# Grouped-query attention on one core: V in 8 KB pieces, 32-row score tiles, 64x64 PV tiles, and a longer TensorE loop

## The chip, the core and the metric

The kernel runs on one core of one Trainium2 chip. The metric is device time in microseconds (us), the median of a few runs. One further execution was recorded by the profiler; its record (the trace, summed up in the page of the profile) is what durations and waits are read from. The engines are PE (TensorE matmuls; PEld its weight loads), DVE (VectorE), ACT (ScalarE), POOL (GpSimd) and SP (SyncE, which here only issues DMAs). Sixteen DMA engines move the data.

## The reference

There are 16 batches, 32 query heads, 8 key/value heads, 16 queries a head, 2048 keys, head size 128, all in bf16. Four query heads share one key/value head.

```python
k = jnp.repeat(k, 4, axis=1); v = jnp.repeat(v, 4, axis=1)
scores = jnp.einsum("bhqd,bhkd->bhqk", q, k) * D ** -0.5
p = softmax(scores, axis=-1)
out = jnp.einsum("bhqk,bhkd->bhqd", p, v)
```

So 128 key/value heads (16 x 8) each meet 64 query rows (4 heads x 16 queries). K and V are 67.1 MB each; q and the output are 2.1 MB each.

## The kernel before, in words

**Tiling.** Four key/value heads make a quad Q (32 quads). K comes by quad, 2 MB at a time, 16 KB in each of 128 partitions (`load_k`, L311). V comes by pair of heads p (64 pairs), 1 MB at a time, as two runs of 4 KB in each partition, one for each head of the pair (`load_v`, L318). The work goes in 64 steps. Step n handles one half of the keys (1024) of all four heads of quad n//2 as far as the scores go, and one pair of heads as far as exp and PV go.

**What a step does on each engine.**
- DVE turns K by 32x32 blocks, two STREAM_TRANSPOSEs a step (`kt`, L558-566), which gives the tile KT; there are two KT buffers. It then reads the scores out of PSUM, scales and negates them, and takes the row minimum on the way (`negated`, L571-579), two instructions a step. At odd steps it also makes the exp bias (L581), at even steps a reciprocal (L568).
- PE computes the scores S(n) (`scores`, L391-406): 16 matmuls of 512 columns in tiles of 64 rows by 128 columns. The weights hold q for two heads with zeros where head and key do not belong together; two tiles run side by side. The four PSUM banks of S_ps hold one step only, so S(n) waits for `negated` of step n-1 (`sem_max`) and for KT (`sem_kt`).
- ACT takes exp (L674), one instruction of 128x2048 a pair, and copies the turned probabilities out of PSUM (L683), two a pair.
- PE turns the probabilities of a pair by eight 128x128 transposes in two halves (`p_turn`, L410: "PT"), and multiplies by V ("PV", L429 for the helper in the loop, L483 and L489 outside). A pair with an even number is done as 16 matmuls with 128x128 weights and 256 moving columns, of which half is thrown away (`both_heads`); an odd one as 32 matmuls in 128x64 tiles with 128 columns.
- ACT scales the result and writes it to SBUF (L697, L701: "norm"); SP stores it (L344).

**Queries.** q is laid out by POOL with a mask (L255, 28 parts), turned by PE in float32 (L392, four transposes a part) and copied by ACT (L664). Inside the loop, POOL also copies a quad's part to a fixed place (L294).

**The order.** PE's order is written out: PV(p-4), PT(p-2), S(p+2), and at every second step a part of q. PE and DVE run loops on the chip: PE 23 turns of two steps (L509, registers computed at the head of a turn: L510-521, waits L525-526), DVE 9 turns of six steps. ACT's program is straight. SP issues in one order (L351-367): at t, K of quad t/2 if t is even (after the K buffer three quads back was turned), V of pair t-6 (after PV of pair t-14; from pair 50 on one t later, `VLATE`), and the store of pair t-14. There are 3 K buffers and 8 V buffers. V of the last pair comes in two pieces (keys 0-11 and 12-15 of each partition's 16).

**The end.** The last five pairs are scaled by DVE (L655) and the last four use banks of S_ps, so that the last exps, PTs and PVs follow one another closely (L206-217).

Of the kernel before, what the change touches and what calls it, by code (L numbers as in the profile page):

```python
# [12 lines left out]
NV = 8  # L13
# [3 lines left out]
NO = 12  # L17
NOG = 4
NQ = 2
NSTAGE = 3  # L20
VLAG = 6
VLATE = 50
PVLAG = 4
SLAG = 14
QLOAD = (0, 1, 5)
QLEAD = 13
QAHEAD = 6
LOOP = (3, 26)
QUNIT = 2
EVBASE = 4  # L30
NMBASE = 6
QTBASE = 1
Q4BASE = 1
VBASE = 16
HEAD = 40
RING = 6
VLOOP = (3, 30)
VHEAD = 140
EXPBASE = 3
LASTV = ((0, 12), (12, 16))  # L40
NFAST = 8
NLATE = 5


def both_heads(p, NP):
    return p < NP - NFAST and p % 2 == 0


def bass_standalone__gqa_softmax__sampling_kernel(
# [10 lines left out]
    G = B * Hkv  # L60
    NP = G // 2
    NQD = NP // 2
    J = Sk // 128
    assert J == 16 and NP % 8 == 0
    NQC = NP // 8
# [6 lines left out]
    ident4 = sb("ident4", [128, 128], F32)  # L72
    mask = sb("mask", [128, 4], F32)
    Kn = [sb(f"Kn{i}", [128, 4 * J * 128], BF16) for i in range(NK)]
    v_base = -(-nc.sbuf_base // 32) * 32
    Vb = sb("Vb", [128, NV, 2, J, 128], BF16)
    KT = [sb(f"KT{i}", [128, 2 * J * 64], F32) for i in range(NKT)]
    Qn = [sb(f"Qn{i}", [128, 8, 128], BF16) for i in range(NQ)]
    Q4 = sb("Q4", [128, 4, 4, 4, 64], BF16)
    QTq = Q4[:, 3, :, :, :].rearrange("p j r c -> p (j r c)").rearrange("p (b n e) -> p b n e", b=2, e=2)  # L80
    QT = [sb(f"QT{i}", [128, 2, 1024], F32) for i in range(2)]
    Sneg = [sb(f"Sneg{i}", [128, Sk], F32) for i in range(NS)]
    P = [sb(f"P{i}", [128, Sk // 2], F32) for i in range(2)]
    PT = [sb(f"PT{i}", [128, J // 2, 128], F32) for i in range(NPT)]
    Osb = [sb(f"O{i}", [128, 128], BF16) for i in range(NO)]
# [11 lines left out]
    def o_done(p):  # L97
        return sem_o[p // NOG % (NO // NOG)], 16 * NOG * (p // NO)

# [4 lines left out]
    iota_m = iota_m.bitcast(I32)  # L104

    S_ps = ctx.enter_context(nc.psum_tensor("S_ps", [128, Sk], F32))
    ST_ps = ctx.enter_context(nc.psum_tensor("ST_ps", [128, NSTAGE * 512], F32))
    O_ps = ctx.enter_context(nc.psum_tensor("O_ps", [128, 512], F32))
# [3 lines left out]
    sem_v = [sem(f"sem_v{i}") for i in range(NV)]  # L112
    sem_vl = [sem(f"sem_vl{i}") for i in range(2)]
    sem_q = [sem(f"sem_q{i}") for i in range(NQ)]
    sem_o = [sem(f"sem_o{i}") for i in range(NO // NOG)]
    sem_kt = sem("sem_kt")
    sem_qa = sem("sem_qa")
    sem_qb = sem("sem_qb")
    sem_q4 = sem("sem_q4")
    sem_qt = sem("sem_qt")  # L120
    sem_qe = sem("sem_qe")
    sem_max = sem("sem_max")
# [3 lines left out]
    sem_stq = sem("sem_stq")  # L126
# [3 lines left out]
    sem_ev = [sem(f"sem_ev{i}") for i in range(2)]  # L130
    sem_nm = sem("sem_nm")
# [5 lines left out]
    vf = v.rearrange("b h s d -> (b h) (s d)").rearrange("g (a x) -> a g x", a=128)  # L137

    pe_prog, act_prog = [], []
    M0, M1 = LOOP  # L140
    NQP = 4 * NQC
    assert M0 >= QUNIT and M1 % 2 == 0 and M1 + QAHEAD <= NQP
    bank_used = [None] * NSTAGE

    def pe_op(*op):
        pe_prog.append(op)

    def q_part(k):
        pe_op("Q", k)
        act_prog.append(("qe", k))  # L150

    def turn(j):
        for h in range(2):
            pe_op("PT", j, h)
            act_prog.append(("pe", j, h))

    def pt_slot(p):
        return p % 2 if p < 2 * M1 - 2 else p % NPT

    for k in range(4):  # L160
        q_part(k)
    pe_op("S", 0)
    pe_op("S", 1)
    for p in range(2 * M1):
        if p == 2 * M0:
            pe_op("loop")
        m, h = divmod(p, 2)
        if p >= 4:
            pe_op("PV", p - 4)
            act_prog.append(("norm", p - 4))  # L170
        act_prog.append(("exp", p))
        if p >= 2:
            turn(p - 2)
        pe_op("S", p + 2)
        if m < QUNIT:
            for k in ((4,), (5,), (6, 7), ())[p]:
                q_part(k)
        elif h == 0:
            q_part(m + QAHEAD)
    pe_op("end")  # L180

    p = 2 * M1
    turn(p - 2)
    pe_op("S", p + 2)
    act_prog.append(("exp", p))
    pe_op("PV", p - 4)
    act_prog.append(("norm", p - 4))
    turn(p - 1)
    if M1 + QAHEAD < NQP:
        q_part(M1 + QAHEAD)  # L190
    p += 1
    pe_op("S", p + 2)
    act_prog.append(("exp", p))
    pe_op("PV", p - 4)
    act_prog.append(("norm", p - 4))
    turn(p - 1)
    turn(p)
    for p in range(2 * M1 + 2, NP - 2):
        pe_op("S", p + 2)
        act_prog.append(("exp", p))  # L200
        pe_op("PV", p - 4)
        act_prog.append(("norm", p - 4))
        turn(p)
        if p % 2 == 0 and p // 2 + QAHEAD < NQP:
            q_part(p // 2 + QAHEAD)
    for p in range(NP - 2 - PVLAG, NP - NLATE):  # L206
        pe_op("PV", p)
        act_prog.append(("norm", p))
    act_prog.append(("exp", NP - 2))
    act_prog.append(("exp", NP - 1))  # L210
    for p in range(NP - NLATE, NP - 3):
        pe_op("PV", p)
    turn(NP - 2)
    pe_op("PV", NP - 3)
    turn(NP - 1)
    pe_op("PV", NP - 2)
    pe_op("PV", NP - 1)

    banks, stage_of, free_of = 0, {}, {}
    for op in pe_prog:  # L220
        if op[0] not in ("Q", "PT"):
            continue
        if op[0] == "Q":
            bank, done = (op[1] % NSTAGE if op[1] < 4 else 2), ("q", op[1] + 1)
            banks = 0
        elif op[1] < max(NP - 8, 2 * M1 - 2):
            bank, done = op[2], (op[2], EVBASE + op[1] + 1)
        else:
            bank, done = banks % NSTAGE, (op[2], EVBASE + op[1] + 1)
            banks += 1  # L230
        stage_of[op], free_of[op] = bank, bank_used[bank]
        bank_used[bank] = done

    def stage_ap(op):
        return ST_ps[:, 512 * stage_of[op]:512 * (stage_of[op] + 1)]

    def copies(n):
        return QUNIT < n <= M1

    def o_ap(p):  # L240
        if p < NP - 4:
            return O_ps[:, 0:128]
        x = p - (NP - 4)
        return S_ps[:, 512 * x:512 * x + 128]

    def q_wide(c):
        return Qn[c % NQ][:, :, :].rearrange("p j (b x) -> p b j x", b=2)

    def lay_part(eng, k):
        c, i = divmod(k, 4)  # L250
        b, x = divmod(i, 2)
        src = q_wide(c)[:, b, 4 * x:4 * (x + 1), :].unsqueeze(2).to_broadcast([128, 4, 4, 64])
        by = mask[:, :].unsqueeze(1).unsqueeze(3).to_broadcast([128, 4, 4, 64])
        region = i if c < 2 else 0
        return eng.tensor_tensor(Q4[:, region, :, :, :], src, by, op=ALU.mult)  # L255

    with nc.Block() as block:

        @block.gpsimd
        def _(gp):  # L260
# [15 lines left out]
            def part(k):  # L276
                c, i = divmod(k, 4)
                if i == 0:
                    gp.wait_ge(sem_q[c % NQ], 16 * (c // NQ + 1))
                gp.wait_ge(sem_stq, k - 3 if c < 2 else 5 if k == 8 else k)  # L280
                ins = lay_part(gp, k)
                if c < 2:
                    ins.then_inc(sem_qb, 1)
                else:
                    ins.then_inc(sem_q4, 1 + (Q4BASE if k == 8 else 0))

            def copy(n):
                c, i = divmod(n, 4)
                gp.wait_ge(sem_s, 2 * n)
                if i == 0 or n == QUNIT + 1:  # L290
                    gp.wait_ge(sem_qe, 4 * c + 4)
                if n == QUNIT + 1:
                    gp.wait_ge(sem_stq, 8)
                gp.tensor_copy(  # L294
                    QTq[:, :, :, :].rearrange("p b n e -> p b (n e)").bitcast(I32),
                    QT[c % 2][:, :, 256 * i:256 * (i + 1)].bitcast(I32),
                ).then_inc(sem_qt, 1 + (QTBASE if n == QUNIT + 1 else 0))

            for k in range(4, QUNIT + QAHEAD + 1):
                part(k)  # L300
            copy(QUNIT + 1)
            for m in range(QUNIT, M1):
                if m + QAHEAD + 1 < NQP:
                    part(m + QAHEAD + 1)
                if copies(m + 2):
                    copy(m + 2)
            for k in range(M1 + QAHEAD + 1, NQP):
                part(k)

        @block.sync  # L310
        def _(sp):  # L311
            def load_k(n):
                s = n % NK
                if n >= NK:
                    sp.wait_ge(sem_kt, 4 * (n - NK) + 4)
                sp.dma_start(Kn[s][:, :], kf[n]).then_inc(sem_k[s], 16)  # L316

            def load_v(p):  # L318
                s = p % NV
                if p >= NV:  # L320
                    sp.wait_ge(sem_pv, p - NV + 1)
                if p < NP - 1:
# [28 lines left out]
            for t in range(NP + SLAG + 1):  # L351
# [14 lines left out]
                if 0 <= t - SLAG < NP:  # L366
                    store(t - SLAG)
# [363 lines left out]
```

## Time and profile before

| what | before |
|---|---|
| median of 3 runs | 338.88 us (338.87 to 341.11) |
| the profiled execution, its own time | 338.73 us |
| its span, first to last instruction | 336.9 us |
| K's turns, DVE L562 | 128 x 1219 ns = 151.0 us busy |
| `negated`, DVE L573 | 128 x 1207 ns = 150.1 us busy |
| exp, ACT L674 | 64 x 2002 ns = 128.1 us busy |
| PSUM copies of PT, ACT L683 | 128 x 590 ns = 68.8 us busy |
| mean DMA rate | 411 GB/s |
| instruction fetches, queue q8 | 8 packets, 0.13 MB |

"Busy" counts the time in which an instruction of the group ran; the mean of one is the duration of one instruction, and where two tiles run side by side the mean of one matmul is longer than the distance from one to the next. The span is 1.83 us shorter than the profiled execution's own time. The profile gives for each group of instructions its idle time before it and what ended that, and a view of stretches of time gives each engine's busy time in them. In the text, "neg" is `negated`, and "E61" is the moment when neg of step 61 has ended, 315.5 us in this trace.

### The profile page before, as it was taken

How to read it: one execution, taken by the hardware profiler on the slowest of the kernel's cores; microseconds unless marked ns; L12 is line 12 of the kernel's file. 1: busy time of each engine (PE TensorE's matmuls, PEld its weight loads, DVE VectorE, ACT ScalarE, POOL GpSimd, SP SyncE). 2: the span in 40 equal slices, each digit the busy share in tenths (PEclk: the TensorE clock that was granted, in tenths of full speed). 3: DMA queues.
4: the chain of work that ended last, by engine and by line, in shares of the span. 5: the costliest groups of instructions: out<-in, count | busy, mean ns of one | idle time of the engine just before them, and what ended most of it. 6: DMA issues, size and time to landing. Idle time of an engine off the chain costs nothing.

```text
span 336.9 us, 7946 instructions
## 1 busy us (share of the span) xinstructions
PE 299.8 (89%) x3264; PEld 172.9 (51%) x2752; DVE 304.7 (90%) x457; ACT 245.9 (73%) x376; POOL 69.7 (21%) x64
## 2 busy tenths in 40 slices
PE   3466899999999999999998998889898879999885
PEld 3012456655566555665555456455465445555564
DVE  1788999999999999999998999989899999999941
ACT  3124887888888898888876877767867787877873
POOL 2802022221222222222122222022221200000000
PEclk9998999999999999999999999999999999999999
DMA  7999999999999999999999999999999999999996
GB/s 294 443 413 431 414 410 408 418 424 426 420 413 413 423 424 422 417 411 421 426 427 416 410 417 424 425 418 422 409 422 425 430 416 424 418 411 416 413 412 226
DMA packets 32670, 138.60 MB, mean 411 GB/s; under 512 B 10896, under 2 KB 11152, under 8 KB 28560
## 3 DMA queue, kind: packets, MB, share of 16 engines
q1 hardware_dynamic: 32656, 138.42, 100.6%
q8 instruction: 8, 0.13, 0.2%
q14 instruction: 6, 0.05, 0.0%
HBM read 136.31 MB, written 2.10 MB: 411 GB/s over the span
## 4 chain that ended last, share of the span: by engine, by line
DMA 39%; PE 32%; DVE 21%; ACT 3%; issue 2%; SPq 2%; DVEq 0%; ACTq 0%
DMA Kn<-in_k_dram 25%; DMA Vb<-in_v_dram 14%; DVE Sneg L573 11%; DVE KT L562 10%; PE O_ps L429 9%; PE S_ps L406 8%; PE S_ps L376 7%; PE ST_ps L414 6%; PE ST_ps L392 2%; ACT P L674 1%; SPq L349 1%; ACT PT L683 1%; ACT QT L664 0%; PE S_ps L489 0%; SPq L316 0%
## 5 line engine op out<-in xcount | busy, mean ns | idle before, releaser
L562 DVE STREAM_TRANSPOSE KT<-Kn 128x1024 f32<-128x1024 f32 x128 | 151.0, 1219 | 9.0 <-DMA Kn<-in_k_dram 9.0
L573 DVE TENSOR_SCALAR_CACHE_REDUCE Sneg<-S_ps 128x1024 f32<-128x1024 f32 x128 | 150.1, 1207 | 8.5 <-PE S_ps L376 8.4
L674 ACT ACTIVATE P<-Sneg,nbias 128x2048 bf16<-128x2048 f32 x64 | 128.1, 2002 | 31.7 <-DVE nbias L582 15.7
L255 POOL TENSOR_TENSOR Q<-Qn,mask 128x1024 bf16<-128x1024 bf16 x28 | 52.9, 1894 | 135.4 <-PE ST_ps L392 128.9
L429 PE MATMUL O_ps<-Vb,PT 128*64 (+1 forms) x1104 | 68.8, 238 | 11.3 <-DMA Vb<-in_v_dram 10.2
L406 PE MATMUL S_ps<-KT,Q 64*128 64x512 bf16 x384 | 74.8, 386 | 0.0
L376 PE MATMUL S_ps<-KT,Q 64*128 64x512 bf16 x384 | 74.2, 383 | 0.0
L429 PEld LDWEIGHTS O_ps<-Vb,PT 128*64 128x64 bf16 (+1 forms) x1104 | 55.6, 106 | 35.2 <-issue 27.9
L683 ACT ACTIVATE PT<-ST_ps 128x512 f32<-128x512 f32 x128 | 68.8, 590 | 3.0 <-PE ST_ps L414 2.2
L414 PE MATMUL ST_ps<-ident,P 128*128 128x128 f32 x512 | 68.2, 276 | 1.5 <-ACT PT L683 1.2
L414 PEld LDWEIGHTS ST_ps<-ident,P 128*128 128x128 f32 x512 | 56.3, 141 | 5.9 <-ACT P L674 2.2
L697 ACT ACTIVATE O<-O_ps,rrec 64x128 bf16<-64x128 f32 x56 | 20.3, 362 | 38.2 <-PE O_ps L429 30.9
L406 PEld LDWEIGHTS S_ps<-KT,Q 64*128 64x128 bf16 x384 | 18.6, 93 | 49.7 <-issue 38.2
L406 PE MATMUL S_ps<-KT,QT 64*128 64x512 bf16 x128 | 28.2, 423 | 13.5 <-DVE Sneg L573 9.8
L392 PEld LDWEIGHTS ST_ps<-ident,Q 128*128 128x128 f32 x128 | 15.2, 153 | 25.4 <-issue 25.4
L376 PE MATMUL S_ps<-KT,QT 64*128 64x512 bf16 x128 | 28.2, 422 | 0.0
L392 PE MATMUL ST_ps<-ident,Q 128*128 128x128 f32 x128 | 22.2, 306 | 6.6 <-DVE Q L605 5.4
L294 POOL COPY Q<-QT 128x512 int32<-128x512 int32 x24 | 14.6, 610 | 58.8 <-PE S_ps L376 58.8
L664 ACT ACTIVATE QT<-ST_ps 128x512 f32<-128x512 f32 x32 | 19.3, 603 | 9.8 <-PE ST_ps L392 9.8
L406 PEld LDWEIGHTS S_ps<-KT,QT 64*128 64x128 bf16 x128 | 7.7, 99 | 34.1 <-issue 29.5
L701 ACT ACTIVATE O<-O_ps,rrec 128x128 bf16<-128x128 f32 x31 | 11.7, 378 | 2.4 <-PE O_ps L489 2.3
L674 ACT ACTIVATION_READ_ACCUMULATOR P<-Sneg,nbias 128x1 f32 x64 | 12.0, 188 | 0.0
(25 smaller groups left out, 71.6 us busy)
## 6 DMA issues: line engine op xcount, KB each, us to landing
Kn<-in_k_dram SPq DMA_DIRECT2D x32, 2048.0 KB, 18.6
Vb<-in_v_dram SPq DMA_DIRECT2D x63, 1024.0 KB, 16.9
Qn<-in_q_dram SPq DMA_DIRECT2D x8, 256.0 KB, 14.7
out_dram<-O SPq DMA_DIRECT2D x64, 32.0 KB, 16.1
Vb<-in_v_dram SPq DMA_DIRECT2D x1, 768.0 KB, 12.8
Vb<-in_v_dram SPq DMA_DIRECT2D x1, 256.0 KB, 12.5
```

The source lines that it names most:

```text
L255: return eng.tensor_tensor(Q4[:, region, :, :, :], src, by, op=ALU.mult)
L376: return pe.add_instruction(mybir.InstMatmult(name=nc.get_next_instruction_name(), engine=mybir.EngineType.PE, ins=[pe.lower_ap(rhs), pe.l ...
L392: ins = pe.transpose(dst[:, 128 * j:128 * (j + 1)], src[:, j, :], ident4[:, :])
L406: ins = pe.matmul(s_ap, w, x, start=(acc == 0), stop=(acc == 3))
L414: ins = pe.transpose(dst[:, 128 * t:128 * (t + 1)], ptile[:, 128 * x:128 * (x + 1)], ident4[:, :])
L429: return pe.add_instruction(mybir.InstMatmult(name=nc.get_next_instruction_name(), engine=mybir.EngineType.PE, ins=[x, pe.lower_ap(w, for_ ...
L562: dve.transpose(KT[n % NKT][:, :].rearrange("p (t b g e a) -> p e g t b a", t=J // 4, b=2, g=4, e=2)[:, e], Kn[Q % NK][:, :].bitcast(F32). ...
L573: ins = dve.tensor_scalar(Sneg[p % NS][:, 1024 * x:1024 * (x + 1)].rearrange("p (t a m) -> p t a m", t=4, m=8), S_ps[:, 1024 * y:1024 * (y ...
L664: act.activation(QT[c % 2][:, i // 2, :].rearrange("p (a x j) -> p x a j", x=2, j=4)[:, i % 2], stage_ap(("Q", k)).rearrange("p (j a) -> p ...
L674: act.activation(P[p % 2][:, :].bitcast(BF16), Sneg[p % NS][:, :], ACT.Exp, bias=col(nbias, p), scale=-1.0, accum_out=col(rowsum, p),).the ...
L683: act.activation(PT[slot][:, 4 * h:4 * (h + 1), :].rearrange("p t q -> p (t q)"), stage_ap(("PT", p, h)), ACT.Copy,).then_inc(sem_ev[h], 1 ...
L697: ins = act.activation(Osb[p % NO][rows, :], O_ps[rows, 128 * g:128 * (g + 1)], ACT.Copy, scale=col(rrec, p)[rows])
```

## The change

- V comes in 64 pieces of 1 MB as before, but each partition receives one run of 8 KB: a head lies in 64 partitions, 32 keys in each. A piece is a pair of heads; two pieces fill one buffer, which holds a quad, and there are 4 such buffers. A buffer is loaded again after both PVs of the quad that used it; both pieces must have landed before the quad's first PV. `VLATE` goes. V of the last quad comes in three pieces of 1, 0.75 and 0.25 MB.
- The scores use tiles of 32 rows by 64 columns, one head each, four tiles side by side: 32 matmuls of 512 columns a step, no zeros in the weights.
- PT and PV go by halves h of the 32 keys, over all four heads of a quad: PT(h) is still eight transposes, PV(h) is 64 matmuls with 64x64 weights and 128 columns, in four tiles. The exps of both pairs of a quad come before its first PT.
- q is turned eight quads' worth at a time (32 bf16 matmuls with 32 columns against a small matrix `fold`, in two groups of 16), once in eight steps; POOL's layout is four instructions for each of these blocks, its copies to the fixed place go, and ACT's copies of q are 16 in place of 32. QT is one buffer.
- PE's program is a head of five steps, a loop of seven turns of eight steps, and a tail. The order in a step is S(p+2), [q], PV(p-5), PT(p-1). At the head of a turn 23 registers are computed. In the loop all waits of S, q and PV are made by the sequencer before it passes on the instructions.
- Stores are by quad, two DMAs of 32 KB. ACT scales all quads but parts of the last two.

The core of the diff (NT = 64 halves, NQD = 32 quads):

```diff
-NV = 8
+NV = 4
-PVLAG = 4
-SLAG = 14
+PVLAG = 5
+SLAG = 16
+TURNS = 7
-LASTV = ((0, 12), (12, 16))
+LASTV = ((0, 16), (16, 28), (28, 32))
...
+    def pe_step(p):
+        ops = [("S", p + 2)]
+        if p >= PVLAG and (p + 3) % 8 == 0:
+            ops += [("Q", (p + 3) // 8, b) for b in range(2)]
+        if p >= PVLAG:
+            ops.append(("PV", p - PVLAG))
+        if p >= 1:
+            ops.append(("PT", p - 1))
+        return ops
+    head = [("Q", 0, 0), ("Q", 0, 1), ("S", 0), ("S", 1)]
+    for p in range(PVLAG):
+        head += pe_step(p)
+    L = NT - 4
+    tail = [("S", NT - 1), ("PV", L - 4), ("PV", L - 3), ("PT", L), ("PT", L + 1), ("PV", L - 2), ("PV", L - 1),
+            ("PV", L), ("PV", L + 1), ("PT", L + 2), ("PT", L + 3), ("PV", L + 2), ("PV", L + 3)]
+    act_prog = [("qe", 0, 0), ("qe", 0, 1)]
+    for p in range(NT - 3):
         act_prog.append(("exp", p))
...
+        if p > PVLAG and (p - PVLAG) % 2 == 1:
+            act_prog += [("norm", (p - PVLAG) // 2, x) for x in range(2)]
+        if p >= 1:
+            act_prog += [("pe", p - 1, i) for i in range(2)]
+    N = NQD - 1
+    act_prog += [("exp", L + 1), ("norm", N - 3, 0), ("norm", N - 3, 1)]
+    act_prog += [("pe", h, i) for h in (L, L + 1) for i in range(2)]
+    act_prog += [("norm", N - 2, 0), ("norm", N - 2, 1), ("exp", L + 2), ("exp", L + 3)]
+    act_prog += [("pe", L + 2, 0), ("pe", L + 3, 0), ("norm", N, 0)]
...
+                n, c = divmod(p, 2)
+                s = n % NV
+                if n >= NV and c == 0:
+                    sp.wait_ge(sem_pv, 2 * (n - NV) + 2)
+                if n < NQD - 1:
+                    dst = Vb[s][:, c, :, :].rearrange("a j d -> a (j d)")
+                    sp.dma_start(dst, vf[p]).then_inc(sem_v[s][c], 16)
...
-                if 0 <= t - VLAG < VLATE:
+                if 0 <= t - VLAG < NT:
                     load_v(t - VLAG)
-                if VLATE <= t - VLAG - 1 < NP:
-                    load_v(t - VLAG - 1)
...
+                    for j in range(8):
+                        for e in range(2):
+                            z = 2 * j + e
+                            ins = pe.matmul(dst[:, 32 * z:32 * (z + 1)], src[:, j, b, e, :], mv, start=True, stop=True)
...
+                    for acc in range(4):
+                        b, e = divmod(acc, 2)
+                        for u in range(2):
+                            for g in (0, 2, 1, 3):
+                                rows = slice(32 * g, 32 * (g + 1))
+                                at, y = 64 * (g // 2), g % 2
+                                s_ap = S_ps[at:at + 64, 512 * (2 * y + u):512 * (2 * y + u + 1)]
...
+                        w = pt[:, j // 2, j % 2]
+                        for c in range(2):
+                            for x in range(2):
+                                rows = slice(64 * x, 64 * (x + 1))
+                                ins = pe.matmul(
+                                    o_ap(n, x)[64 * c:64 * (c + 1), :], w[rows, c], Vb[n % NV][rows, c, key, :],
+                                    start=(key == 0), stop=(key == 31),
+                                )
...
+            for slope, values in ((8, range(1, 21)), (16, (16,)), (4, (8,)), (2, (4,))):
+                for value in values:
+                    regs[slope, value] = pe.alloc_register(f"r_{slope}_{value}")
+            with nc.Fori(0, TURNS, 1, engines=[PE], head_slot={PE: HEAD}) as m:
+                for (slope, value), r in regs.items():
+                    pe.reg_alu(r, m, slope, ALU.mult)
+                    pe.reg_alu(r, r, value, ALU.add)
+                for p in range(PVLAG, PVLAG + 8):
+                    for op in pe_step(p):
+                        emit(op, True)
```

## The prediction

> **What bounds the kernel now.** I read the engines' busy time first, then the costliest groups, then a table by stages, then what DVE waits for, and last the timeline of the end.
>
> ```profile
> PE 299.8 (89%) x3264; PEld 172.9 (51%) x2752; DVE 304.7 (90%) x457; ACT 245.9 (73%) x376; POOL 69.7 (21%) x64
> ...
> q1 hardware_dynamic: 32656, 138.42, 100.6%
> ...
> L562 DVE STREAM_TRANSPOSE KT<-Kn 128x1024 f32<-128x1024 f32 x128 | 151.0, 1219 | 9.0 <-DMA Kn<-in_k_dram 9.0
> ```
>
> Three things are full at once: DMA (packets take all of the span), DVE and PE. Which one ends last differs by stage. In the table by stages the columns are the stretch, its length, busy time of PE, PEld, DVE, ACT, POOL, PE's clock, the DMA share and GB/s:
>
> ```profile
> 31.00:172.00 141.00, 137.41 (x1463) 79.09 (x1220) 140.19 (x211) 114.78 (x178) 35.10 (x29) 1.00 1.02 418
> 172.00:290.00 118.00, 105.57 (x1133) 61.45 (x950) 109.80 (x163) 89.57 (x140) 23.09 (x19) 1.00 1.02 420
> 290.00:325.00 35.00, 32.58 (x405) 19.48 (x348) 32.78 (x53) 26.80 (x43) 0.00 (x0) 1.00 1.03 416
> ```
>
> From 31 to 172 us DVE is busy 99.4% of the time: steps follow each other every 4.68 us (neg of step 5 starts at 41.04, of step 33 at 172.13, 28 steps). From 172 to 290 it waits for K:
>
> ```profile
> DVE KT L562 <- DMA Kn<-in_k_dram: 5.3, 11, 0.9
> DVE Sneg L573 <- PE S_ps L376: 2.4, 8, 0.4
> ```
>
> Those 22 steps (neg 34 at 177.00, neg 56 at 289.84) take 112.8 us where 22 x 4.68 = 103.0 would do: 10 us lost to the DMA. After that DVE is full again, and K of the last quad, complete at 310.5 us by the landings, is just in time for the turn at 310.89. Then comes the end:
>
> ```profile
> 310.89 2.35 DVE L562 STREAM_TRANSPOSE KT<-Kn 128x1024 f32<-128x1024 f32 x2
> ...
> 325.80 1.99 ACT L674 ACTIVATE P<-Sneg,nbias 128x2048 bf16<-128x2048 f32 x1
> ...
> 327.79 1.99 ACT L674 ACTIVATE P<-Sneg,nbias 128x2048 bf16<-128x2048 f32 x1
> ...
> 333.36 1.09 PE L489 MATMUL S_ps<-Vb,PT 128*64 128x128 bf16 x32 [0.26 <-DMA Vb<-in_v_dram]
> ...
> 334.49 0.35 DVE L655 TENSOR_SCALAR O<-S_ps,rrec 128x128 bf16<-128x128 f32 x1 [0.93 <-PE S_ps L489]
> ```
>
> So the path is: the DMA stream up to the last K, DVE to E61 (315.5), then exp, PT, PV, norm and store, 21.4 us from E61 to the end at 336.9. The last V, complete at 333.9, is almost as late.
>
> **Part 1: V in 8 KB runs.** From the landings between 60 and 310 us, K takes 4.917 us per 2 MB when it follows V (8 packets of 16 KB an engine: 614 ns each) and V 2.547 us per MB (16 packets of 4 KB: 159 ns each). A straight line through both has 7 ns a packet and 0.037 ns a byte, so 8 KB takes 311 ns and a piece 2.488 us: 0.059 us less, 3.7 us over 63 pieces. Ends: nothing, and 0.088 a piece (K's rate per byte), 5.5 us. I take the line, since 8 KB lies between its two rows. The Trainium skill (DMA: Bandwidth & Descriptors, "Why small descriptors are slow (HBM only)") puts the fixed cost at about 3 cycles a packet; at its 850 MHz that is 3.5 ns, an estimate by which the pieces would save 1.8 us in all and the sum below would end 1.7 us later. But without `VLATE` piece 55 now goes ahead of the last K. Ahead of it lie 56 x 2.488 = 139.3 us of V where 55 x 2.547 = 140.1 lay: the last K lands only 0.8 us earlier, and E61 by this is 314.7. The DMA gain falls behind K31, where the last V (333.9 - 3.7 = 330.2) has no one waiting for it.
>
> **Part 2: PE's steps.** Scores: 16 matmuls before, two side by side, every 225 ns (206.34, 206.57, 206.79): 1.8 us. Now 32, four side by side: the same 8 x 225 ns if four run like two. PV: 1.91 us (even, at 203.16) or 1.09 (odd, at 208.37; by the starts in the trace 56 ns from one pair of tiles to the next); now 16 rounds of four tiles, 0.9 us at the odd form's 56 ns. Ends: 0.9 and 1.8 us (two at a time); I take 0.95, because two row tiles (scores) and two column tiles (odd PV) each run side by side in this trace. PT stays 1.09. A step is then 1.85 + 0.95 + 1.09 + 0.3 of gaps = 4.2 us, under DVE's 4.68. DVE's and ACT's instructions keep shape and number (new strides only; I cost them at nothing, within DVE's own spread of 1201 to 1247 ns for a turn); ACT's norms fall from 56 x 0.362 + 31 x 0.378 to 62 x 0.378, off the path. POOL's work hides behind eight steps.
>
> **Part 3: once a turn.** Two things delay a score and thereby DVE. (a) q: 32 weight loads and matmuls in one step. The nearest rows are 28 ns a tile in odd PV and 109 ns from one float32 transpose to the next, 0.9 to 3.5 us; I take 1.5, as the weights are bf16 but 128 wide. That step is 4.2 + 1.5 = 5.7 us; DVE bears S about 0.25 us late (neg to neg 2.16 us on PE's side against 2.37 of turns), so 0.8 us lost. (b) The loop's head: register and branch instructions start when the second half of PT is let go, 0.53 us before PE is free. In this trace the branch with its neighbour takes 0.37 us and 31 additions took 0.80 (205.41 to 206.21), so 46 operations take 1.1, with a wait 1.57 in all: the next score is 0.55 late, 0.3 lost. If each pair went singly (0.133 us each) it would be 3.06 and 2.2 lost. Together 1.1 us a turn, 7.7 us in all. Without its K waits E61 would be 315.5 - 10.0 = 305.5; with the turns 313.2. K (314.7) is still later and hides it.
>
> **Part 4: the end.** The order changes there, and I go through it from E61. S(63) can start at neg 62's end, 4.8 to 6.75; PV56 and PV57 follow to 8.7; PT60 and PT61, two banks emptied by ACT in 0.53 us each, to 11.3; PV58, PV59 to 13.2. In ACT's order norm of quad 29 stands ahead of the last two exps and waits for PV59: 13.3 to 14.1. So the exps run 14.1 to 18.1, where before they ran from 10.3 to 14.3, with the bias ready at 9.6. Then PT62, PT63, their copies (ACT and DVE side by side), PV62, PV63: 22.45; norm 22.9; store as before, 2.1 after it: 25.0 where it was 21.4. Ends: 21.4 (ACT is never held) and 30 (PV at 1.8 us six times).
>
> **Sum.** 314.7 + 25.0 = 339.7 us of span; plus 1.83 us around it in the profiled execution: 341.5. That execution (338.73) lies 0.15 under the median shown, which I leave out.
>
> **Rivals.**
> *Slower: the turns.* At each turn's end PE stands still for longer than 1.1 us. For it: seven turns, each with a lump of q and a jump back over some 1,600 matmuls and loads; DVE has no room in 31 to 172 us. Before, PE fetched a 16 KB packet of its program about every 260 instructions (at 41.06 and 52.44 us 261 and 502 had started) and none while its short loop ran. If the long body is fetched anew, the wait is at least one such packet (1.04 us) a turn; q at 109 ns a pair adds 2.0. With 3 us a turn, E61 is 305.5 + 21 = 326.5 and the time 353.3. It decides from 1.35 us a turn on, where K stops hiding it. The Trainium skill (Runtime: NRT & Kernel Launch, "Instruction fetch mechanics") says that a taken branch to a target outside the resident window waits for a fetch, which would make this rival the likely one; its figure of 2048 instructions for PE would let the body stay. No run shows yet which holds.
> *Slower by far: tiles two at a time.* If PV takes 1.8 us, a step is 5.05 us and PE bounds: 58 x 0.37 = 21 more, the turns no longer hidden (2.6 each), tail 30: about 378. If scores go two at a time (two of the four tiles write one bank), 1.8 us more a step: over 400. Against: the two-way rows above.
> *Faster: the end holds.* If ACT is not held and V runs at K's rate per byte, K31 is 2.4 us earlier, E61 313.1, the tail 21.4: 336.3. At best the last V sets the end: 328.4 + 3.0 + 1.83 = 333.2.
> *The change does not do what it says:* 8 KB costs as much per byte as 4 KB. Then K31 lands 2.5 us later than before (one more piece ahead), E61 is 318 and the time 344.8; I count this with the forecast.
>
> **How the numbers follow.** Forecast 46% (338.5 to 345, from Part 1's ends and 1 us either way in the tail), turns 26% (345 to 358), tiles 13% (above 370), faster 15% (333 to 338.5). The range 335 to 358 leaves out the tiles and about a third of the faster case. About 1% is what a measurement of this kernel can tell from no change: under 335.5 lies a third of the faster case and little else, 7%; over 342.3 lie two fifths of the forecast, the turns and the tiles, 56%; 37% remain.
>
> **What would show it.** Step right: V's landings 2.49 us apart; PV's 64 matmuls in under 1 us; neg to neg 4.68 us between turns and some 1 us more at each; exp of step 62 behind ACT's norm. Wrong: K waits of DVE gone or doubled; PE's idle before S at a turn above 1.5 us; a score above 2.1 us; packets of the instruction queue in every turn.

## The result and the profile after

| | before | after |
|---|---|---|
| median | 339.12 us (338.87 to 341.11, 4 runs) | 348.21 us (347.71 to 348.93, 4 runs) |
| the profiled execution, its own time | 338.73 us | 348.93 us |
| its span | 336.9 us | 347.1 us |
| last K has landed | 310.50 us | 311.65 us |
| E61 (neg of step 61 has ended) | 315.5 us | 316.3 us |
| from E61 to the end | 21.4 us | 30.8 us |

The change makes the kernel slower: ratio 1.0256 (95% interval 1.0213 to 1.0300). Almost all of it lies behind E61.

The page of the changed kernel: busy time of the engines, the queue of data, and the group of K's turns (now L397).

```profile
PE 274.4 (79%) x6912; PEld 159.5 (46%) x5888; DVE 304.7 (88%) x457; ACT 223.6 (64%) x332; POOL 82.0 (24%) x42
...
q1 hardware_dynamic: 24720, 138.42, 96.6%
...
L397 DVE STREAM_TRANSPOSE KT<-Kn 128x1024 f32<-128x1024 f32 x128 | 151.0, 1219 | 10.1 <-DMA Kn<-in_k_dram 10.1
```

PE has 25 us less to do and twice as many instructions. DVE's work is the same to the tenth, and DVE was the bound. The 16 DMA engines spend 335.3 us on packets (96.6% of 347.1) where they spent 338.9 (100.6% of 336.9). By stages, with the columns as before:

```profile
31.00:172.00 141.00, 121.01 (x2974) 69.48 (x2495) 137.35 (x205) 100.53 (x149) 38.95 (x14) 0.98 1.01 419
172.00:290.00 118.00, 100.08 (x2600) 59.41 (x2214) 113.22 (x171) 84.59 (x129) 28.88 (x11) 1.00 1.02 423
```

In the first stretch DVE lost 2.8 us to PE's start and to the first turn of its loop. In the second it does 3.4 us more than before (113.22 against 109.80): its waits for scores, 2.4 us before, are gone, and those for K fell from 5.3 to 4.4 us. K still paces it in the end: up to 220 us DVE makes up what it had lost, and from there on it waits 0.6 to 0.7 us for K at every second step (view of DVE's waits in that stretch: sum, times, longest).

```profile
DVE KT L397 <- DMA Kn<-in_k_dram: 4.4, 7, 0.7
```

The timeline of the end shows where the 9.4 us came from. Columns: start, busy time, engine, line, operation and tiles, count; in brackets the idle time ahead of it and what ended it.

```profile
327.49 0.42 PE L369 MATMUL O_ps<-Vb,PT 64*64 64x128 bf16 x15
...
329.55 1.80 PE L369 MATMUL O_ps<-Vb,PT 64*64 64x128 bf16 x113 [1.64 <-issue]
...
331.14 0.39 PE L369 MATMUL S_ps<-Vb,PT 64*64 64x128 bf16 x14
331.47 0.63 ACT L532 ACTIVATE O<-O_ps,rrec 128x128 bf16<-128x128 f32 x2 [3.28 <-PE O_ps L369]
331.99 2.00 ACT L516 ACTIVATE P<-Sneg,nbias 128x2048 bf16<-128x2048 f32 x1
...
333.97 2.00 ACT L516 ACTIVATE P<-Sneg,nbias 128x2048 bf16<-128x2048 f32 x1
...
334.37 2.18 PE L369 MATMUL S_ps<-Vb,PT 64*64 64x128 bf16 x114 [2.84 <-issue]
...
336.48 1.97 PE L338 MATMUL ST_ps<-ident,P 128*128 128x128 f32 x8
...
339.61 1.93 PE L369 MATMUL O_ps<-Vb,PT 64*64 64x128 bf16 x124
...
343.26 0.25 PE L369 MATMUL O_ps<-Vb,PT 64*64 64x128 bf16 x4 [1.72 <-issue]
```

Three times PE stands still in the middle of a PV (L369), behind 15 matmuls of PV58, 14 of PV60 and 124 of PV62 and PV63, and nothing that the profile shows holds it: "issue". Between the first and the second stop lie 127 matmuls with 127 weight loads, 254 instructions; between the second and the third, 254 matmuls and PTs, twice that. The view of the DMA queues says what comes in such steps. PE's queue is q8. From 95 to 325 us, where the loop runs its turns two to seven, it has no packet at all; q14, the other queue marked "instruction", has its three packets in run 7 below too, where PE does not stop:

```profile
q1 hardware_dynamic: 17313, 96.98, 101.6%
q14 instruction: 3, 0.02, 0.0%
```

and from 325 us to the end it is back, with four packets of 16 KB:

```profile
q1 hardware_dynamic: 2561, 2.80, 35.8%
q8 instruction: 4, 0.07, 1.2%
```

By the trace they start at 327.01, 331.90, 335.47 and 340.90 us, and the three stops end 2.54, 2.47 and 2.36 us after the first, second and fourth. Some 1.3 us after the second stop PE's granted clock goes to 0.5, from 335.64 to 339.05, and PT62 at 336.48 takes 1.97 us where a PT took 1.09.

### The profile page after: what moved, and what is told of

Read it like the earlier page. It is cut to its first block, busy times and chain, and to the rows that moved or that the text cites. A ratio compares the mean times of both kernels' runs of the same rounds, so it can differ in the third digit from the quotient of the medians.

```text
span 347.1 us, 14217 instructions
## 1 busy us (share of the span) xinstructions
PE 274.4 (79%) x6912; PEld 159.5 (46%) x5888; DVE 304.7 (88%) x457; ACT 223.6 (64%) x332; POOL 82.0 (24%) x42
## 3 DMA queue, kind: packets, MB, share of 16 engines
q1 hardware_dynamic: 24720, 138.42, 96.6%
## 4 chain that ended last, share of the span: by engine, by line
DVE 47%; DMA 21%; PE 14%; SPq 11%; issue 5%; ACT 1%; DVEq 0%; ACTq 0%
DVE Sneg L410 25%; DMA Kn<-in_k_dram 21%; DVE KT L397 21%; SPq L213 5%; SPq L240 4%; PE S_ps L315 4%; PE S_ps L271 4%; PE O_ps L369 3%; PE ST_ps L338 2%; SPq L227 1%; PE S_ps L369 1%; ACT O L532 0%; PE S_ps L338 0%; DVE rrec L406 0%; SPq L204 0%
## 5 line engine op out<-in xcount | busy, mean ns | idle before, releaser
L397 DVE STREAM_TRANSPOSE KT<-Kn 128x1024 f32<-128x1024 f32 x128 | 151.0, 1219 | 10.1 <-DMA Kn<-in_k_dram 10.1
L315 PE MATMUL S_ps<-KT,QT 32*64 32x512 bf16 x1024 | 110.1, 399 | 54.3 <-DVE Sneg L410 49.3
L516 ACT ACTIVATE P<-Sneg,nbias 128x2048 bf16<-128x2048 f32 x64 | 128.5, 2008 | 23.0 <-DVE nbias L419 22.9
L166 POOL TENSOR_SCALAR Q<-Qn,mask 128x1024 bf16<-128x1024 bf16 x28 | 79.1, 2845 | 171.6 <-PE ST_ps L294 165.9
L271 PE MATMUL S_ps<-KT,QT 32*64 32x512 bf16 x1024 | 110.1, 395 | 0.0
L315 PEld LDWEIGHTS S_ps<-KT,QT 32*64 32x64 bf16 x1024 | 36.0, 106 | 121.2 <-issue 108.4
L369 PEld LDWEIGHTS O_ps<-Vb,PT 64*64 64x64 bf16 x3968 | 57.6, 107 | 38.7 <-issue 38.5
L369 PE MATMUL O_ps<-Vb,PT 64*64 64x128 bf16 x3968 | 67.8, 218 | 4.8 <-issue 4.8
L532 ACT ACTIVATE O<-O_ps,rrec 128x128 bf16<-128x128 f32 x61 | 19.2, 364 | 33.6 <-PE O_ps L369 33.6
L507 ACT ACTIVATE QT<-ST_ps 128x512 bf16<-128x512 f32 x16 | 8.7, 594 | 8.8 <-PE ST_ps L294 8.8
L294 PE MATMUL ST_ps<-fold,Q 128*128 128x32 bf16 x256 | 7.8, 178 | 5.3 <-DVE Q L166 5.3
L294 PEld LDWEIGHTS ST_ps<-fold,Q 128*128 128x128 bf16 x256 | 7.0, 98 | 9.8 <-issue 9.8
L410 DVE DVE_READ_ACCUMULATOR Sneg<-S_ps 128x1 f32 x128 | 10.6, 83 | 0.0
L369 PE MATMUL S_ps<-Vb,PT 64*64 64x128 bf16 x128 | 2.6, 236 | 2.8 <-issue 2.8
(23 smaller groups left out, 13.5 us busy)
```

The source lines that it names most:

```text
L166: eng.tensor_scalar(Q4[:, :, :, r, :].rearrange("p j b x -> p (j b) x"), src, mask[:, r:r + 1], None, op0=ALU.mult,).then_inc(sem_q4, 1)
L271: return pe.add_instruction(mybir.InstMatmult(name=nc.get_next_instruction_name(), engine=mybir.EngineType.PE, ins=[pe.lower_ap(rhs), pe.l ...
L294: ins = pe.matmul(dst[:, 32 * z:32 * (z + 1)], src[:, j, b, e, :], mv, start=True, stop=True)
L315: ins = pe.matmul(s_ap, w, x, start=(acc == 0), stop=(acc == 3))
L369: ins = pe.matmul(o_ap(n, x)[64 * c:64 * (c + 1), :], w[rows, c], Vb[n % NV][rows, c, key, :], start=(key == 0), stop=(key == 31),)
L397: ins = dve.transpose(KT[n % NKT][:, :].rearrange("p (t b g e a) -> p e g t b a", t=8, b=2, g=2, e=2)[:, e], Kn[Q % NK][:, :].bitcast(F32) ...
```

## The experiments

Three theories. *Program fetch*: the tail is straight code in which PE runs through 256 instructions in about 2.0 us (128 matmuls of PV with their loads took 1.98 us at 323.13), faster than the next 256 arrive. *Order of ACT*, the forecast's own term: its norm of quad 29 holds the last two exps. *DMA*: the place of the last K in the stream and the size of V's runs. Twelve kernels; each time is a median, each ratio is to the kernel before, run beside it.

**1. ACT's last exps first.**

```diff
-    act_prog += [("norm", N - 2, 0), ("norm", N - 2, 1), ("exp", L + 2), ("exp", L + 3)]
+    act_prog += [("exp", L + 2), ("exp", L + 3), ("norm", N - 2, 0), ("norm", N - 2, 1)]
```

> ACT's last two exps go ahead of its norm of quad 29, nothing else changes. Theory 'order of ACT' (the forecast's own term for the end): the exps start when the copies of PT61 are done, 3.8 us sooner, and the time falls by 3.5 to 3.8 us, to about 344.5. Theory 'program fetch' (PE stands still at each new block of straight-line code): the exps do start 3.8 us sooner, but PE comes to PT62 only after PV61, whose two stops of 1.6 and 2.8 us stay, so the time falls by 0 to 0.6 us, to about 347.8. Theory 'DMA': no change.

Measured: 348.45 us, ratio 1.0265 (1.0238 to 1.0291), no gain. The exps did start at 328.20, 3.8 us sooner; PE came to PT62 at 336.59, behind PV61 with both stops (1.64 and 1.60 us in this run, and half clock between them). Taken alone, the order of ACT is worth nothing here.

**2. Fewer instructions in the tail.** `for j in range(8 if few else 16)` in PV56 to PV61.

> PV of steps 56 to 61 does only half of its keys (32 of 64 matmuls each, with their weight loads), so that part of the work is left out: 384 instructions of PE less in the tail, 3.3 us of matmul time. Theory 'program fetch': of four program packets in the tail two or three are left, the first stop comes behind PV59 and no longer ahead of the norm of quad 29, and the end comes 4 to 6 us sooner, 342 to 344. Theory 'order of ACT': only the four PVs ahead of the norm count, 2.2 us, 346; the stops stay where they are in time.

Measured: 342.90 us, 1.0109 (1.0079 to 1.0138): 5.3 us less, for 3.3 us of matmuls. E61 was 315.75, 0.6 us sooner, and the tail 25.2 us. Of the stops one is left, in PV60, and it is over before the exps are:

```profile
326.95 0.38 PE L370 MATMUL S_ps<-Vb,PT 64*64 64x128 bf16 x14
327.26 0.62 ACT L533 ACTIVATE O<-O_ps,rrec 128x128 bf16<-128x128 f32 x2 [0.52 <-PE O_ps L370]
...
328.61 0.91 PE L370 MATMUL S_ps<-Vb,PT 64*64 64x128 bf16 x50 [1.27 <-issue]
```

As program fetch had it. PV62 and PV63 ran through without a stop, but at half clock for the most part, in 3.00 us.

**3. The same code, 40 instructions earlier in its blocks.** `HEAD = 0` where it was 40.

> The loop's head is put at slot 0 of a block of the program where it stood at slot 40, so that every block ends 40 instructions later in the tail; work, order and waits are the same. Theory 'program fetch': the stop that came 4 matmuls (8 instructions) before the end of PV63 falls behind it and 1.7 us go, 346.5; the stops in PV58 and PV60 come about 20 matmuls later in their PV, of the same length. Theories 'order of ACT' and 'DMA': nothing changes, 348.2.

Measured: 348.34 us, 1.0241 (1.0216 to 1.0266), 347.1 to 351.1: the time missed the expectation, the places did not. In its profiled run (351.06 us) PV58 broke behind 35 matmuls where it was 15, PV60 behind 34 where it was 14, and the last two PVs did not break:

```profile
343.52 2.00 PE L369 MATMUL O_ps<-Vb,PT 64*64 64x128 bf16 x128
```

The tail took 27.8 us (E61 321.4, end 349.1), 3.0 us less. But the blocks had moved in the head and the loop's first turn as well: PE stood still for 5.1 us from 47.72 us, where the changed kernel's idle time was 1.73 us, the buffers of K and V filled up, the stream fell to 355 GB/s between 50 and 70 us, and every K from K8 on landed about 5 us later. So the stops follow the blocks of the program, here too, and what one gains at the end can be lost at the start.

**4. V one place later from piece 50 on**, as `VLATE` had it.

> V pieces from 50 on are issued one place later, as in the kernel before, so that one piece less lies ahead of the last K. Theory 'DMA' (the last K sets the end of step 61): K of the last quads lands 2.5 us sooner, the K waits of DVE after step 54 (0.7 us at every second step) go, the end of neg 61 comes 2.1 to 2.8 us sooner and so does the end: about 345.7. Rival: DVE is bound by its own work there and at most the last wait goes: 0.7 us, 347.5. The tail stays 30.8 us by either.

Measured: 348.08 us, 1.0255 (1.0228 to 1.0282), no gain. The last K landed at 309.15, 2.50 us sooner, and E61 was 314.20, 2.1 us sooner, both as expected; but the tail grew to 31.6 us:

```profile
328.67 0.39 PE L372 MATMUL S_ps<-Vb,PT 64*64 64x128 bf16 x14
...
333.26 3.11 PE L372 MATMUL S_ps<-Vb,PT 64*64 64x128 bf16 x114 [4.21 <-issue]
```

The second stop is 4.21 us. Its packet started only at 330.66, 1.6 us after PE had stopped, while V was still streaming.

**5. V in 4 KB runs.** Two DMAs a piece, of 16 keys each, and waits for 32.

> Every V piece but those of the last quad comes as two DMAs with one run of 4 KB in each partition, where it was one DMA with a run of 8 KB; bytes, buffers and order are the same. From the landings of K7 to K27 the changed kernel takes 0.073 us less a quad than the kernel before. Theory 'packets cost by the straight line' (0.059 us a piece): K of the last quad lands 3.3 us later and the time rises by 3.3 us to 351.5. Theory 'small price' (all of the 0.073 us a quad): 2.0 us later, 350.2. Rival 'the size of a run is worth nothing': 348.2, within 0.7 us.

Measured: 352.82 us, 1.0403 (1.0378 to 1.0429). The last K landed at 315.85, 4.2 us later. From K7 to K27 the 20 quads took 206.59 us, 204.11 in the changed kernel, 205.56 before: 0.124 us a quad for the size, 0.062 a piece. (1.4 us of the 4.2 came in the first turn.) More than expected, since the kernel before is no measure of it: with the same runs of 4 KB its stream was 0.05 us a quad quicker. Run 12 is the control.

**6. The last two quads' V not loaded.** `if n >= NQD - 2: return` in `load_v`; PE's waits for these pieces go with it.

> V of the last two quads is not loaded (PV60 to PV63 work on what earlier quads left in the buffers), so that part of the result is another; PE's program is the same. The DMA stream then ends at about 324 us and the program packets of the tail meet quiet queues. Theory 'the packet queues behind the data' (in the tail a packet starts about 1.1 us after PE enters the block before it when the queues are quiet, and 2.4 to 3.6 us when V is streaming): both stops ahead of PT62 become 1 to 1.6 us shorter and the end comes 2 to 3 us sooner, 345.2 to 346.2. Rival 'a fetch takes what it takes, whatever the data do': stops of 1.6 and 2.8 us as before, time 348.2 within 0.5.

Measured: 345.68 us, 1.0197 (1.0178 to 1.0217), 2.5 us less, as expected. The first packet came 7.9 us after E61 (10.7 in the changed kernel), the first stop is gone and the second is 1.56 us:

```profile
327.30 1.98 PE L367 MATMUL O_ps<-Vb,PT 64*64 64x128 bf16 x128
329.11 0.39 PE L367 MATMUL S_ps<-Vb,PT 64*64 64x128 bf16 x14
...
331.05 1.81 PE L367 MATMUL S_ps<-Vb,PT 64*64 64x128 bf16 x114 [1.56 <-issue]
```

So data hold a program packet up, and the stops ahead of the exps were that long because V was still coming. The last stop, for which the queues are quiet in both kernels, stays (2.02 us).

**7. The tail as an eighth turn of the loop.** All work is done; what does not exist is jumped over. ACT's list changes with it: the last two exps stand ahead of the norm of quad 29.

```diff
+                    elif z <= 4:
+                        with pe.If_lt(turn, last):
+                            emit(ops[0], True)
+                    emit(pv, True)
```

> The loop of TensorE runs an eighth turn in place of the straight tail; in it the scores, PTs and q that do not exist are jumped over. All work is done; V of the last quad comes in two whole pieces, ACT does the last norms and copies alone, and the order at the end is S63, PV56, PT60, PV57, PT61, PV58, PT62, PV59, PT63, PV60 to PV63. Theory 'program fetch': no program packet after the first turn, no stop of PE in the tail, half clock gone; by the durations of the trace (exps from 11.5 to 15.5 us after the end of neg 61, PT62, PV59, PT63 to 19, four PVs, norm, store) the tail is 26 to 28 us in place of 30.8 although its order is less good, time 343.5 to 346. Rival 'jumps are as dear as the fetch' (each step has a branch): steps get longer than DVE's 4.68 us or each taken jump stops PE for 1 us or more, and the time stays at 348 or rises. Theory 'order of ACT': PT62 comes no earlier than 16 us after the end of neg 61 and the tail stays at 30 us.

Measured: 347.38 us, 1.0258 (1.0229 to 1.0286): the time missed the expectation, the stops did not. From 95 us to the end the trace has no packet of PE's queue, and no stop behind "issue":

```profile
327.02 1.09 PE L350 MATMUL O_ps<-Vb,PT 64*64 64x128 bf16 x64
327.67 2.02 ACT L500 ACTIVATE P<-Sneg,nbias 128x2048 bf16<-128x2048 f32 x1
...
331.81 1.19 PE L319 MATMUL ST_ps<-ident,P 128*128 128x128 f32 x8 [3.70 <-ACT P L500]
...
332.92 1.92 PE L350 MATMUL O_ps<-Vb,PT 64*64 64x128 bf16 x64
...
334.77 1.71 PE L319 MATMUL ST_ps<-ident,P 128*128 128x128 f32 x8
```

All PVs up to PV58 are done at 328.1; but now PE stands still for 3.7 us with nothing to do until the exps are there, the half clock (332.67 to 336.08) follows that idle time, and the tail is 29.2 us. The gain is that small because the order of a turn has its price: PT62 starts 15.7 us after E61 (20.2 in the changed kernel), but five PVs stand behind it in place of two, and from PT62 to the end it is 13.5 us in place of 10.7. The jumps cost nothing that can be seen: DVE is busy 76.72 of the 77 us from 95 to 172, exactly as without them. PE waits for DVE at most scores, so a cost that fits in these waits (0.71 us at 321.01) would not show.

**8. The eighth turn and the late V.**

> The eighth turn in place of the tail, and V pieces from 50 on issued one place later, so that the last K lands 2.5 us sooner. With the late V alone the end of neg 61 came 2.1 us sooner but PE's second stop grew from 2.8 to 4.2 us and took it back. Theory 'program fetch': without stops the 2.1 us stay, 341.5 to 344. Rival 'the last V sets the end': V63 lands at 334 as before and PV62 waits for it; then the same time as with the eighth turn alone.

Measured: 345.79 us, 1.0172 (1.0137 to 1.0207). The gain of the late V, 1.6 us, now stays; the level is that of run 7, so higher than expected.

**9. The same, and ACT relieved.** DVE, idle by then, copies PT60, PT61 and half of PT62 and PT63 and scales quad 28 and half of the last two; ACT goes straight to the exps.

```diff
+    act_prog += [("free",), ("exp", L + 1), ("exp", L + 2), ("exp", L + 3)]
```

> The eighth turn and the late V, and in the tail DVE copies PT60, PT61 and half of PT62 and PT63 and scales quad 28 and half of quads 30 and 31, so that ACT goes from exp 61 straight to the last two exps. With the eighth turn alone ACT held them 2.5 us behind the bias and PE then stood still for 3.7 us and ran at half clock. Theory 'with the program resident ACT's order and load set the end': the exps start with the bias, 2.3 us sooner, and the half clock goes with PE's long idle time, 1.5 us: 341.5 to 343. Rival 'the last V sets the end': V63 lands at about 332 and PV62 cannot start ahead of that; 343 or more, with PE waiting for DMA.

Measured: 340.68 us, 1.0051 (1.0031 to 1.0070), 5.1 us less than run 8 and better than expected:

```profile
323.20 2.00 ACT L523 ACTIVATE P<-Sneg,nbias 128x2048 bf16<-128x2048 f32 x1 [2.44 <-DVE nbias L419]
...
325.20 1.99 ACT L523 ACTIVATE P<-Sneg,nbias 128x2048 bf16<-128x2048 f32 x1
...
327.34 1.09 PE L320 MATMUL ST_ps<-ident,P 128*128 128x128 f32 x8 [1.16 <-ACT P L523]
328.03 0.60 ACT L531 ACTIVATE PT<-ST_ps 128x512 f32<-128x512 f32 x1 [0.75 <-PE ST_ps L320]
328.36 1.09 PE L351 MATMUL O_ps<-Vb,PT 64*64 64x128 bf16 x64
```

The exps start with the bias, PE's idle time ahead of PT62 is 1.16 us and the clock stays whole until PE is done. E61 is 313.7, 1.0 us sooner than in run 8, and the tail 25.2 us, 4.1 us shorter. The 1.0 us does not come from this edit as far as the trace shows: the last K landed 1.05 us sooner (308.58 for 309.63), and the edit changes only the tail. The last V has landed at 331.8, before PV62 at 333.17, so it does not set the end. This is the best version tried; it is still half a per cent above the kernel before.

**10. The last store from two queues.** ACT issues its second half.

> As the kernel with DVE in the tail, but ACT issues the second half of the last quad's store, where SP issued both one after the other. In the changed kernel the last landing came 2.7 us after the norm, in the kernel before 1.7 us, with one DMA behind the last norm. Theory 'the second issue costs it': 0.6 to 1.0 us less than the kernel with DVE in the tail. Rival: the landing itself is slower, no change.

Measured: 340.80 us, 1.0055 (1.0036 to 1.0074), the same as run 9. The last landing came 0.3 us sooner (338.05 for 338.39), too little for the expectation.

**11 and 12. Controls of run 5**: two DMAs a piece with runs of 8 KB, by halves of the partitions and by even and odd ones.

```diff
-                    sp.dma_start(dst, vf[p]).then_inc(sem_v[s][c], 16)
+                    for lo in (0, 1):
+                        dst = Vb[s][lo:128:2, c, :, :].rearrange("a j d -> a (j d)")
+                        sp.dma_start(dst, vf[p][lo:128:2, :]).then_inc(sem_v[s][c], 16)
```

> A control of the 4 KB runs: the changed kernel with every V piece as two DMAs too, but of 64 partitions each with runs of 8 KB. Theory 'the size of the run costs': as the changed kernel, 348.2 within 0.8, K of the last quad at about 311.7. Rival 'two DMAs a piece cost': as with the 4 KB runs, K of the last quad at about 315.8 and 352 to 353.

> The control of the 4 KB runs again: two DMAs for every V piece with runs of 8 KB, one for the even and one for the odd partitions, since two DMAs of 64 neighbouring partitions took 575 us. Theory 'the size of the run costs': as the changed kernel, K of the last quad at about 311.7 and 348.2 within 0.8. Rival 'two DMAs a piece cost': as with the 4 KB runs, K of the last quad at about 315.8 and 352 to 353. If DMAs of 64 partitions are slow whichever these are, the time is far above 400 and the control says nothing.

Measured: the halves took 575.26 us and say nothing on the question. Even and odd: 348.80 us, 1.0285 (1.0271 to 1.0299), the last K at 312.36, and 204.16 us from K7 to K27. That is the changed kernel's pace (204.11): the size of the run costs, the number of DMAs does not. The stretch from 172 to 290 us of run 12 and then of run 5:

```profile
172.00:290.00 118.00, 99.73 (x2596) 59.04 (x2212) 112.89 (x171) 84.12 (x127) 28.96 (x11) 1.00 1.02 423
```

```profile
172.00:290.00 118.00, 96.64 (x2507) 57.39 (x2128) 109.73 (x165) 81.77 (x124) 29.16 (x11) 1.00 1.02 419
```

## Why the prediction was right in direction and short in size

The forecast was 341.5 us in a range of 335 to 358, slower the likeliest sign. Measured: 348.2. Its span was 339.7 and came out 7.4 us longer: 1.6 in E61, 5.8 behind it. That the range holds the time is in part luck: 348.2 lies above the forecast's own 338.5 to 345, in the band (345 to 358) that stood for the turns, and the turns cost nothing. The tail's 30.8 us lie above the upper end of 30 as well.

**What bounds the kernel**: right. DVE and the stream set everything up to E61, and 25 us less of PE work did not bring it forward.

**Part 1, E61: 314.7 predicted, 316.3 measured.** The straight line gave 0.059 us a piece for 8 KB; runs 5 and 12 give 0.062, so the price was right. But between the two kernels only 0.073 us a quad came, 0.036 a piece. Over 56 pieces that is 1.3 us less than forecast, most of the 1.6. What took the other 0.05 us a quad was not found. The last V landed at 333.12 us, where 330.2 was forecast. The lost `VLATE` was judged rightly: run 4 moved the last K by 2.50 us. The weighing of the Trainium skill (DMA: Bandwidth & Descriptors, "Why small descriptors are slow (HBM only)") can now be closed: 0.062 us over 8 packets an engine is 7.7 ns a packet, and the estimate of 3.5 ns from its 3 cycles is half of that.

**Part 2: right, with PV 0.1 us dearer.** Scores go four side by side every 225 ns, PV's 64 matmuls take 1.09 us (0.95 taken), a float32 PT 1.09:

```profile
160.36 0.42 PE L271 MATMUL S_ps<-KT,QT 32*64 32x512 bf16 x4
160.58 0.42 PE L315 MATMUL S_ps<-KT,QT 32*64 32x512 bf16 x4
...
161.16 1.09 PE L369 MATMUL O_ps<-Vb,PT 64*64 64x128 bf16 x64
```

**Part 3, 1.1 us a turn: wrong, without consequence.** q took 0.9 us (165.90 to 166.80) where 1.5 was taken, and neg followed neg every 4.61 to 4.78 us, at the turns and at q's step to within 0.04 us as elsewhere. Only the first turn cost something: stops of 1.14 and 1.61 us behind program packets at 70.02 and 76.97, 1.5 us of DVE's time, regained by K27, which landed 1.3 us sooner than before. Two small sums are off without moving the forecast: 46 operations at 0.80 us for 31 are 1.2 us, not 1.1, and the turns would have decided from 1.31 us each (314.7 less 305.5, over seven), not 1.35.

**Part 4, the tail: 25.0 predicted, 30.8 measured. This is the step that failed.** Times after E61, in us:

| | predicted | changed kernel | run 9 |
|---|---|---|---|
| PT61 done | 11.3 | 11.2 | 11.4 |
| PV59 done | 13.2 | 15.0 | not on the path |
| norm of quad 29 done | 14.1 | 15.8 | not on the path |
| last two exps done | 18.1 | 19.7 | 13.5 |
| PV63 done | 22.45 | 27.2 | 21.6 |
| last norm done | 22.9 | 27.7 | 22.1 |
| end | 25.0 | 30.8 | 25.2 |

Up to PT61 the working holds to 0.1 us. Then come the first stop (1.6, carried through norm and exps), the second, of which only 0.4 shows beyond the exps, PT62 and PT63 at half clock (3.13 us to PV62 where run 6 took 1.93: 1.2), the third stop (1.7), and a store that takes 3.1 us where 2.1 was taken (1.0): 5.9 in all for the 5.8. Two DMAs now follow the last norm where one did, the second issued 0.64 us behind the first, and from issue to landing it took 1.96 us where the kernel before had 1.67; but run 10, with both issued at once, gained 0.3 us only, so the store's 1.0 stays open for the rest.

The working of Part 4 priced a PV at its matmul time. The rate of program packets, one in about 260 instructions, stood in the prediction, but was used for the loop alone. The tail's PVs have 128 instructions each, where those of the kernel before had 64 in the same 1.09 us. That kernel's trace even showed it in small: a packet at 329.65, and PE back 2.54 us later, after 0.44 us of "issue" in PV62:

```profile
332.19 0.92 PE L489 MATMUL S_ps<-Vb,PT 128*64 128x128 bf16 x25 [0.44 <-issue]
```

The hold of the exps by ACT's norm was real and predicted to 1.7 us, yet run 1 shows that it was worth nothing while PE was stopped: the stops hid it. Run 7 takes away both the stops and this hold. PT62 then comes 4.5 us sooner behind E61, and 2.9 of them are lost behind it to the order of a turn and the half clock. Run 9 goes further, with DVE doing part of ACT's work: of its 5.1 us against run 8, 2.0 lie ahead of PT62, 2.1 behind it and 1.0 in E61, which the edit does not explain. A tail without stops in the changed kernel's own order was not run, so what the stops alone cost, with everything else as it was, is a sum read from the trace and not a measured time.

**Rivals.** *The turns* fell: no program packet from 95 to 325 us. By the 2048 instructions that the Trainium skill (Runtime: NRT & Kernel Launch, "Instruction fetch mechanics") gives for PE the loop may stay, and it stays; its rule that crossing a block is mostly hidden does not hold in this tail, where three crossings stopped PE for 6.2 us. *Tiles two at a time* fell by the 225 ns. *The end holds* fell. *8 KB as dear as 4 KB* fell as stated, but more than a third of the gain is missing (0.036 us a piece came of 0.059).

## What to carry to other kernels

A smaller tile doubles the instructions of the same work: for the straight parts of a program, count instructions per microsecond beside matmul time, since PE went on only about 2.5 us after a program packet had started, and 256 instructions of PV last 2.0 us. Code that a loop has already run was free of that here, and a tail can be a turn of the loop with jumps, at the price of the loop's order. Where two things hold the same end, undoing one alone can show nothing (run 1); undo both before calling one harmless.

## What the runs showed of the hardware

- A packet of PE's program started about 1.1 us after PE had gone on into a new block when V was in (334.37 to 335.47 in the changed kernel), and 2.35 us after it (329.55 to 331.90) or 3.6 us (327.07 to 330.66 in run 4) while V streamed. It is no fixed rule: 1.11 us in run 3 with the last V still coming (334.56 to 335.67), 1.83 us in run 6 without V (331.05 to 332.88). PE went on 2.3 to 2.9 us after the packet's start. That the start of a block is what asks for the packet is read from these times, not shown by itself.
- A loop of about seven blocks of 256 instructions was fetched once, in its first turn (seven packets from 48.44 to 89.31 us, then none up to 325); 9 jumps a turn added nothing that shows beside DVE's 76.72 us of 77 (run 7).
- In the tail the granted clock fell to 0.5, each time for 3.4 us, after idle times of PE of 2.84 us (changed kernel), 3.70 (run 7), 2.02 (run 3) and 1.64 (run 1); it did not after 1.56 (run 6), nor after the changed kernel's own first 1.64. At the start of the changed kernel it was 0.5 for 17 us (18.20 to 35.27). Where the limit lies these runs do not tell.
- With V in DMAs that write 64 neighbouring partitions, alternating between the halves, the kernel moved 241 GB/s in the mean and took 575 us; with the same bytes to even and odd partitions it moved 399 GB/s (run 12). The line of run 11's page:

```profile
DMA packets 25730, 138.67 MB, mean 241 GB/s; under 512 B 11888, under 2 KB 12144, under 8 KB 13680
```
